# Where the softmax denominators of batches 4 to 7 are summed, in a fused attention and SwiGLU kernel on one Trainium2 core

## The chip, the cores and the metric

The kernel runs on one core of a Trainium2 chip. The core has a matrix engine (PE, with the loading of its stationary operand shown as PEld), a vector engine (DVE), a scalar engine (ACT), a general engine (POOL, also called GpSimd) and a queue engine (SP) that here only issues transfers. Each engine works through its own list of instructions in order, and the lists meet through semaphores. Matrix products go to PSUM, which has eight banks per partition. One bank holds 512 float32 values in each of 128 partitions.

The metric is the device time in microseconds (us) of one execution. The profile is of one other execution of the same program, with a span that is a little shorter than its own device time.

## The reference

Two blocks follow each other. The first is an attention with 32 memory slots per head, for 8 batches, 8 heads, 576 positions and a head size of 64:

```python
a = np.exp(phi - np.max(phi, axis=2, keepdims=True))
a = a / (np.sum(a, axis=2, keepdims=True) + 1e-09)      # over the 576 positions
k_m = np.einsum('bhsm,bhsd->bhmd', a, k)
v_m = np.einsum('bhsm,bhsd->bhmd', a, v)
scores = scale * np.matmul(q, k_m.transpose(0, 1, 3, 2))
attn = softmax(scores)                                   # over the 32 slots
out = np.matmul(attn, v_m)
```

The second is a SwiGLU layer over all 4608 tokens: `silu(x @ w_gate) * (x @ w_val) @ w_out`, with 512 model columns and 1536 inner ones. Inputs and output are float32.

What matters here is the division in the second line. For each head and slot one sum over 576 positions, the denominator, scales a row of `k_m` and of `v_m`.

## The kernel before

The kernel works on one batch after the other, in matrix products of bfloat16. For a batch it forms, in this order: the sums over positions ("key sums", though they hold keys and values: `kv_sum`, line 248, into two PSUM banks named `p_kv0` and `p_kv1`); their denominators (`kv_denominators`, line 293); the reciprocals of those (`kv_reciprocal`, line 301, on DVE, into `t_rS`); the scaled sums (`kv_norm`, lines 305 and 317, on DVE, into `t_bkv`); their transpose (`kv_T`, for batches 4 to 7 a transfer that SP issues, line 326). Then come the products of the value part with the two weight matrices (`p_u`, line 525), the scores (line 445), their softmax (multiplication at line 506, into `t_A`), and 24 slots per batch of a gate product and a value product (`p_g` and `p_v`, line 586), with the sigmoid unit on ACT (line 603) and a multiplication on DVE (line 609, into `t_h`). The output products (line 808) use sums of blocks that POOL and DVE prepare (lines 631 and 674).

The order on each engine is written out by hand. Batch b runs its 24 slots, and among these stand the next batch's key sums: `kv_items(b + 1, ...)` is put at slot 6 to 8, and its scaled sums are needed only by the products of `u_three` at slot 19 and by the next batch's scores. With the key sums, PE runs the last of batch b's own `p_u` products, in small tiles of the array (64 rows by 32 columns) that run beside each other. ACT and DVE copy these products out ("copies": at lines 552 and 556); `units` are four output products from a list that is left over.

A denominator is a product with two columns of ones. From batch 3 on POOL adds up the nine parts of exp(phi) first (`phi_sum`, lines 229 to 236: six operations), and leaves the sum as two bfloat16 parts in `t_ehl`, so that PE needs two matrix products for it (line 293), and not nine. Before that POOL waits, by a copy of one element (`wait_for`, line 716), until the softmax multiplication of head group 1 of batch `before` is done. `before` is the batch whose slots are running, so 2 for batch 3, 3 for batches 4 and 5, 5 for batch 6 and 6 for batch 7.

Where the denominators stand depends on the batch. For batches 3, 4, 6 and 7 (`behind`) they come after the key sums and the units, in two free columns (128 and 129) of `p_kv0`, and the reciprocal follows on DVE behind a copy of `p_u`. For batch 5 (`own`) they come ahead of the key sums, in a bank of their own, `p_S`, which is given back at once.

PSUM banks are handed out from a list of eight, first in, first out (`bank` and `done`). The order of the list is fixed when the program is built; a matrix product into a bank waits for the last reader of the bank's former contents.

Of the kernel before, what the change touches and what calls it, by code (L numbers as in the profile page):

```python
# [9 lines left out]
FP32 = mybir.dt.float32  # L10
# [4 lines left out]
def kernel(  # L15
# [28 lines left out]
    NG = 2  # L44
# [30 lines left out]
    def bank(shape, dtype, name):  # L75
        tag = free.pop(0)
        t = ps.tile(shape, dtype, tag=tag, name=name)
        held[id(t)] = tag, t
        return t

    def done(*tiles):

        for t in tiles:
            free.append(held.pop(id(t))[0])
# [27 lines left out]
    counted = (2,)  # L112
# [72 lines left out]
    ephis, rSs, bkvs, kTs, es, atts = {}, {}, {}, {}, {}, {}  # L185
# [34 lines left out]
    esums = {}  # L220

    def phi_sum(b, before):

        e = ephis[b].rearrange("p j i m -> p j (i m)")
        wait_for(atts[before, 1][0:1, 0, 0:1])
        t = att.tile([128, 4, 128], FP32, tag="es", bufs=1, name="t_es")
        add = lambda o, x, y: nc.gpsimd.tensor_tensor(out=o, in0=x, in1=y, op=ALU.add)
        add(t, e[:, 0:4], e[:, 4:8])  # L230
        add(t[:, 0:2], t[:, 0:2], t[:, 2:4])
        add(t[:, 0], t[:, 0], t[:, 1])
        add(t[:, 0], t[:, 0], e[:, 8])
        hl = att.tile([128, 2, 128], BF16, tag="ehl", name="t_ehl")
        nc.gpsimd.tensor_copy(out=hl[:, 0], in_=t[:, 0])
        nc.gpsimd.tensor_tensor(out=hl[:, 1], in0=t[:, 0], in1=hl[:, 0], op=ALU.subtract)
        esums[b] = hl
# [3 lines left out]
    def kv_sum(b, p, parts, among={}):  # L241


        w0, w1 = parts[0], parts[-1] + 1
        n = (w1 - w0 + (b in counted)) * D

        def one(i, g, j):
            nc.tensor.matmul(  # L248
                p[g][32 * i:32 * i + 32, 0:n],
                lhsT=phi_of(b, g, j, i),  # L250
                rhs=kv_of(b, slice(64 * g, 64 * g + 64), w0, w1, i, j),
                start=(j == 0),
                stop=(j == JK - 1),
                tile_position=(64 * g, 32 * i),
            )

        jobs = []
        for x, (i, g) in enumerate(TILES):
            at = 4 * x
            for j in range(JK + 1):  # L260
                for n_u, job in enumerate(among.get((i, g), ())):
                    if j == AHEAD[b][g][n_u][i]:
                        jobs.append((at, x, job))
                        at += 224
                if j < JK:
                    jobs.append((at, x, lambda i=i, g=g, j=j: one(i, g, j)))
                    at += 60
        run(x for _, _, x in sorted(jobs, key=lambda t: t[:2]))
# [5 lines left out]
    def kv_denominators(b, p):  # L274

        if b in masked:
            for g in range(NG):
                for j in range(JK):
                    nc.tensor.matmul(
                        p[:, g:g + 1],  # L280
                        lhsT=masked[b][:, j, g].rearrange("p i m -> p (i m)"),
                        rhs=ones1,
                        start=(j == 0),
                        stop=(j == JK - 1),
                    )
            return
        if b in esums:
            hl = esums.pop(b)
            terms = [hl[:, t] for t in range(2)]
        else:  # L290
            terms = [ephis[b][:, j].rearrange("p i m -> p (i m)") for j in range(JK)]
        for n, x in enumerate(terms):
            nc.tensor.matmul(p, lhsT=x, rhs=ones2, start=(n == 0), stop=(n == len(terms) - 1))

    def kv_reciprocal(b, p):
        r = att.tile([128, NG], FP32, tag="rS", name="t_rS")
        if b in counted:
            for g in range(NG):
                nc.vector.reciprocal(out=r[:, g:g + 1], in_=p[g][:, D:D + 1])
        else:  # L300
            nc.vector.reciprocal(out=r, in_=p)
        rSs[b] = r
# [4 lines left out]
    def kv_norm(b, p):  # L307

        t = att.tile([128, 3, 128], BF16, tag="bkv", name="t_bkv")
        flat = t.rearrange("p n x -> p (n x)")  # L310
        o = 2 * D if b in counted else D
        for g in range(NG):
            out = flat[:, 2 * D * g:].rearrange("p (a x) -> p a x", a=2)[:, :, D:2 * D]
            x = p[g][:, 0:2 * o].rearrange("p (a x) -> p a x", a=2)[:, :, 0:D]
            scaled_copy(out, x, rSs[b][:, g:g + 1])
            done(p[g])
        nc.vector.tensor_copy(out=t[:, 0:NG, 0:D], in_=t[:, 0:NG, D:2 * D])
        bkvs[b] = t

    def kv_T(b):  # L320


        kTs[b] = att.tile([128, 3, 128], BF16, tag="kT", name="t_kT")
        t = bkvs.pop(b)
        if b > 3:
            nc.sync.dma_start_transpose(out=kTs[b], in_=t.rearrange("p n x -> p (n x)"))
            return
        p = bank([128, 3, 128], BF16, "p_T")
        for n in (2, 0, 1):
            nc.tensor.transpose(p[:, n], t[:, n], ident)  # L330
        nc.vector.tensor_copy(out=kTs[b], in_=p)
        done(p)

    def kv_items(b, beside=None):


        def run_sums():
            o = 2 * D
            behind = b in esums and b != 5
            own = beside and not behind  # L340
            if own:
                d = bank([128, NG], FP32, "p_S")
                kv_denominators(b, d)
                kv_reciprocal(b, d)
                done(d)
            p = [bank([128, CH], FP32, f"p_kv{g}") for g in range(NG)]
            if beside:
                u, units = beside
                copies = u(lambda x: kv_sum(b, p, (0, 1), x))
                run(copies[:3])  # L350
            else:
                kv_sum(b, p, (0, 1))
            if behind:
                run(copies[3:5])
                units()
                kv_denominators(b, p[0][:, o:o + NG])
            if not own:
                kv_reciprocal(b, p if b in counted else p[0][:, o:o + NG])
            kv_norm(b, p)
            if behind:  # L360
                run(copies[5:])
            if own:
                run(copies[3:])
                units()

        return [run_sums, lambda: kv_T(b)]

    def direct(b, which):
# [344 lines left out]
    def wait_for(x):  # L713

        t = att.tile([1, 1], BF16, tag="mark", bufs=1, name="t_mark")
        nc.gpsimd.tensor_copy(out=t, in_=x)
# [236 lines left out]
    def run(items):  # L953
        for x in items:
            x()
# [155 lines left out]
    for b in range(2, B):  # L1111
        last = b + 1 == B
        exp_tables()
        if b == 2:
# [5 lines left out]
            sums = {n: f for n, f in zip(((1, 1), (0, 2), (1, 2)), late)}  # L1120
# [67 lines left out]
        beside = 0 if last else 2 if quad else min(4, len(backlog))  # L1188
# [5 lines left out]
        if not last:  # L1194
            if b > 2:
                load_qT(b + 1)
            for n in {3: (4, 5), 4: ()}.get(b, (b + 1,)):
                phi_sum(n, b)
            kvs_next = kv_items(b + 1, (u_beside(b), lambda: run(take(2))))
            streams += [  # L1200
                (kvs_next[:1], KV, KV + 2),
                (kvs_next[1:], KV + 2 + 2 * (b == 2), KV + 4 + 2 * (b == 2)),
                ([lambda: (u_three(b + 1), run(take(2)))], 19, 20),
            ]
        spread(*streams)
        flush_mul()
        units, ops = products(b, ("p1", "c11"))
# [35 lines left out]
```

## Time and profile before

| | |
|---|---|
| median of 3 runs | 231.25 us (231.09 to 231.45) |
| the profiled execution, its own device time | 231.05 us |
| span of the profile | 229.3 us, at full granted clock |
| busy share of PE, DVE, ACT, POOL | 96%, 81%, 75%, 66% |
| chain of work that ended last | 87% PE, 9% DMA |
| key sums of batch 4, 5, 6, 7 start at | 101.71, 127.68, 153.79, 177.54 us of the span |
| denominator products of batch 4, 5, 6, 7 start at | 103.26, 127.56, 155.34, 179.09 us |
| POOL done with the sum for batch 4, 5, 6, 7 | 102.32, 106.26, 154.49, 177.98 us |

The profile has a page with the busy time of each engine, the chain of work that ended last (followed back from the last instruction) and the costliest groups of instructions. From the same trace one can ask who waited for whom, and for a list of the instructions in order of time. A row of that list gives the start, the length of the row (of a run of equal instructions: from the first one's start to the last one's end), the engine, the line, the operation, what it writes and reads, and the count. A matrix product's end is modelled, so two rows of PE can overlap; the distance from start to start is what PE took.

### The profile page before, as it was taken

How to read it: one execution, taken by the hardware profiler on the slowest of the kernel's cores; microseconds unless marked ns; L12 is line 12 of the kernel's file. 1: busy time of each engine (PE TensorE's matmuls, PEld its weight loads, DVE VectorE, ACT ScalarE, POOL GpSimd, SP SyncE). 2: the span in 40 equal slices, each digit the busy share in tenths (PEclk: the TensorE clock that was granted, in tenths of full speed). 3: DMA queues.
4: the chain of work that ended last, by engine and by line, in shares of the span. 5: the costliest groups of instructions: out<-in, count | busy, mean ns of one | idle time of the engine just before them, and what ended most of it. 6: DMA issues, size and time to landing. Idle time of an engine off the chain costs nothing.

```text
span 229.3 us, 7221 instructions
## 1 busy us (share of the span) xinstructions
PE 220.2 (96%) x2826; PEld 170.5 (74%) x2826; DVE 186.7 (81%) x423; ACT 171.4 (75%) x365; POOL 151.8 (66%) x207
## 2 busy tenths in 40 slices
PE   6987899999999999999999999999999999999993
PEld 2544476778887876888788887888788878878893
DVE  4246699999977999999997768998999899977832
ACT  2868988988537898988875758978898889677311
POOL 8422737998099759979987788464845494039291
PEclk9999999999999999999999999999999999999999
DMA  6999999999994997999199955995114902202024
GB/s 212 209 210 206 198 207 207 208 258 266 207 195 118 248 279 154 230 204 195 72 219 197 177 175 124 256 226 94 38 56 115 105 0 96 91 0 94 23 92 164
DMA packets 36546, 36.84 MB, mean 161 GB/s; under 512 B 14496, under 2 KB 30880, under 8 KB 36512
## 3 DMA queue, kind: packets, MB, share of 16 engines
q0 software_dynamic: 16272, 22.42, 53.0%
q1 hardware_dynamic: 19568, 13.24, 22.7%
q10 hardware_dynamic: 672, 0.72, 0.9%
q8 instruction: 22, 0.36, 0.6%
q14 instruction: 12, 0.10, 0.1%
HBM read 42.47 MB, written 9.44 MB: 226 GB/s over the span
## 4 chain that ended last, share of the span: by engine, by line
PE 87%; DMA 9%; POOL 2%; issue 0%; ACT 0%; POOLq 0%; ACTq 0%
PE p_g L586 21%; PE p_v L586 21%; PE p_os L808 20%; PE p_oc L808 10%; DMA W<-in_moe_w_val_dram 9%; PE p_oa L808 5%; PE p_u L525 5%; PE p_kv L248 2%; PE p_os L796 1%; PE p_g L445 1%; POOL t_kv L101 1%; POOL t_kv L110 1%; POOL t_q L125 0%; PE p_q L432 0%; POOL W L155 0%
## 5 line engine op out<-in xcount | busy, mean ns | idle before, releaser
L609 DVE TENSOR_TENSOR t_h<-t_sg,p_v 128x288 bf16<-128x288 bf16 x192 | 82.1, 452 | 12.0 <-PE p_v L586 6.8
L586 PEld LDWEIGHTS <-t_U 128*128 128x128 bf16 x768 | 73.8, 98 | 19.9 <-issue 2.8
L603 ACT ACTIVATE t_sg<-p_g 128x288 bf16<-128x288 f32 x192 | 74.3, 420 | 18.4 <-PE p_g L586 12.0
L586 PE MATMUL p_g<-t_A,t_U 128*128 128x288 bf16 x384 | 77.0, 286 | 0.0
L586 PE MATMUL p_v<-t_A,t_U 128*128 128x288 bf16 x384 | 77.0, 286 | 0.0
L808 PEld LDWEIGHTS <-t_S 128*128 128x128 bf16 x384 | 37.3, 98 | 4.6 <-issue 0.2
L674 POOL TENSOR_TENSOR t_S<-t_h 128x512 bf16<-128x512 bf16 x17 | 19.7, 1157 | 23.3 <-DVE t_h L609 22.1
L808 PEld LDWEIGHTS <-t_h 128*128 128x128 bf16 x288 | 27.0, 98 | 7.3 <-issue 3.5
L552 ACT CAST t_U<-p_u 128x512 bf16<-128x512 f32 x50 | 26.4, 606 | 4.1 <-PE p_u L525 4.1
L808 PE MATMUL p_os<-t_T,t_S 128*128 128x256 bf16 x192 | 23.7, 273 | 0.0
L631 POOL TENSOR_TENSOR t_S<-t_S,t_h 128x512 bf16<-128x512 bf16 x17 | 19.6, 1155 | 1.3
L631 POOL TENSOR_TENSOR t_S<-t_h,t_S 128x512 bf16<-128x512 bf16 x16 | 18.4, 1154 | 0.0
L631 POOL TENSOR_TENSOR t_S<-t_h 128x512 bf16<-128x512 bf16 x16 | 18.4, 1152 | 0.0
L525 PE MATMUL p_u<-W,t_kT 64*32 64x512 bf16 (+1 forms) x416 | 16.5, 363 | 1.1 <-DVE t_kT L388 0.6
L556 DVE CAST t_U<-p_u 128x512 bf16<-128x512 f32 x22 | 14.3, 685 | 1.1 <-PE p_u L525 1.1
L808 PE MATMUL p_os<-t_T,t_h 128*128 128x256 bf16 x96 | 14.8, 274 | 0.0
L980 PE MATMUL p_warm<-bones 128*128 128x512 bf16 x44 | 12.6, 424 | 1.7 <-DVE bones L1002 1.7
L386 ACT COPY t_q<-p_os 128x512 f32<-128x512 f32 (+2 forms) x12 | 5.5, 470 | 9.2 <-PE p_os L796 5.1
L808 PE MATMUL p_oc<-t_T,t_S 128*128 128x256 bf16 x96 | 12.1, 273 | 0.0
L808 PE MATMUL p_oa<-WO,t_h 128*128 128x256 bf16 x96 | 11.8, 273 | 0.0
L808 PE MATMUL p_oc<-WO,t_S 128*128 128x256 bf16 x96 | 11.8, 273 | 0.0
L808 PE MATMUL p_os<-WO,t_h 128*128 128x256 bf16 x96 | 11.8, 273 | 0.0
(115 smaller groups left out, 329.4 us busy)
## 6 DMA issues: line engine op xcount, KB each, us to landing
out_dram<-t_o SPq DMA_DIRECT2D x11, 512.0 KB, 3.5
t_kv<-in_k_dram POOLq DMA_DIRECT2D x8, 576.0 KB, 10.7
t_q<-in_q_dram POOLq DMA_DIRECT2D x8, 576.0 KB, 8.2
t_kv<-in_v_dram POOLq DMA_DIRECT2D x8, 576.0 KB, 15.8
t_phi<-in_phi_dram POOLq DMA_DIRECT2D x6, 576.0 KB, 8.4
out_dram<-t_o SPq DMA_DIRECT2D x10, 256.0 KB, 7.4
WO<-in_moe_w_out_dram POOLq DMA_DIRECT2D x3, 512.0 KB, 19.2
W<-in_moe_w_gate_dram POOLq DMA_DIRECT2D x2, 512.0 KB, 16.2
```

The lines of the kernel that those rows point to most:

```text
L248: nc.tensor.matmul(p[g][32 * i:32 * i + 32, 0:n], lhsT=phi_of(b, g, j, i), rhs=kv_of(b, slice(64 * g, 64 * g + 64), w0, w1, i, j), start=( ...
L386: nc.scalar.copy(out=out, in_=in_)
L525: nc.tensor.matmul(p[g][32 * i:32 * i + 32, o:o + n], lhsT=kTs[b][64 * g:64 * g + 64, 2, 32 * i:32 * i + 32], rhs=w_part(w, c, i, g, halve ...
L552: nc.scalar.copy(out=t, in_=p)
L556: nc.vector.tensor_copy(out=t, in_=p)
L586: nc.tensor.matmul(p[:, 0:HALF], lhsT=Us[b, c, g][:, o // 2, which, 128 * (o % 2):128 * (o % 2 + 1)], rhs=atts[b, g][:, r], start=(g == 0) ...
L603: nc.scalar.activation(out=sg, in_=gate[:, 0:HALF], func=AF.Silu)
L609: nc.vector.tensor_tensor(out=dst, in0=sg, in1=val[:, 0:HALF], op=ALU.mult)
L631: eng.tensor_tensor(out=out, in0=x, in1=y, op=ALU.subtract)
L674: eng.tensor_tensor(out=t[:, 0], in0=A21, in1=A22, op=ALU.add)
L808: nc.tensor.matmul(mine[home][:, u], lhsT=lhs(c, m, u), rhs=rhs(c, m), start=fresh and u == 0, stop=(k == 5), skip_group_check=u == 1 or n ...
L980: nc.tensor.matmul(p[:, 0:128 * a], lhsT=bones, rhs=x.to_broadcast([128, a, 128]) if a > 1 else bones, start=True, stop=True,)
```

## The change

The diff is whole:

```diff
@@ phi_sum(b, before)
-        wait_for(atts[before, 1][0:1, 0, 0:1])
+        wait_for(atts[before, b < 4][0:1, 0, 0:1])
@@ kv_items(b, beside), run_sums
             o = 2 * D
-            behind = b in esums and b != 5
-            own = beside and not behind
-            if own:
-                d = bank([128, NG], FP32, "p_S")
-                kv_denominators(b, d)
-                kv_reciprocal(b, d)
-                done(d)
             p = [bank([128, CH], FP32, f"p_kv{g}") for g in range(NG)]
+            sums = p[0][:, o:o + NG]
+            if b > 3:
+                kv_denominators(b, sums)
+                kv_reciprocal(b, sums)
             if beside:
                 u, units = beside
                 copies = u(lambda x: kv_sum(b, p, (0, 1), x))
-                run(copies[:3])
+                n = {3: 5, 5: 3}.get(b, 4)
+                run(copies[:n])
+                if b != 5:
+                    units()
             else:
                 kv_sum(b, p, (0, 1))
-            if behind:
-                run(copies[3:5])
-                units()
-                kv_denominators(b, p[0][:, o:o + NG])
-            if not own:
-                kv_reciprocal(b, p if b in counted else p[0][:, o:o + NG])
+            if b == 3:
+                kv_denominators(b, sums)
+            if b <= 3:
+                kv_reciprocal(b, p if b in counted else sums)
             kv_norm(b, p)
-            if behind:
-                run(copies[5:])
-            if own:
-                run(copies[3:])
+            if beside:
+                run(copies[n:])
+            if b == 5:
                 units()
```

For batches 4, 6 and 7 the two denominator products and the reciprocal move from behind the key sums to ahead of them, into the same two columns of `p_kv0` as before. For batch 5 they stay ahead of the key sums, and move from a bank of their own into those columns. For batches 4 to 7 POOL's sums wait for the softmax multiplication of head group 0, and no longer for that of group 1. The orders of copies and units, and all of batches 2 and 3, are what they were. No instruction is added or removed.

## The prediction

> **What bounds the kernel now.** I read the page first, then the list of waits, then the list of instructions in order of time around each of the four key sums.
>
> ```profile
> span 229.3 us, 7221 instructions
> ...
> PE 220.2 (96%) x2826; PEld 170.5 (74%) x2826; DVE 186.7 (81%) x423; ACT 171.4 (75%) x365; POOL 151.8 (66%) x207
> ...
> PE 87%; DMA 9%; POOL 2%; issue 0%; ACT 0%; POOLq 0%; ACTq 0%
> ```
>
> PE bounds it: the chain is PE from 26.6 us on, when the weights have landed. In the waits PE itself appears with what happens before that, like the first line here; later it waits some hundredths at most:
>
> ```profile
> PE p_warm L980 <- DVE bones L1002: 1.7, 1, 1.7
> ...
> DVE t_rS L301 <- PE p_kv L293: 0.7, 3, 0.2
> ```
>
> The last line (total, times, longest in us) is the only wait that the old place of the denominators makes: DVE idles 0.7 us in three batches. It is DVE's idle time, and PE does not wait for what follows. So a microsecond saved on DVE here is worth nothing, and one that PE loses is lost in full, unless PE loses less later; from 82 us to 223 us I find no wait of PE above 0.03 us that could shrink.
>
> Batch 6 stands for 4 and 7 as well:
>
> ```profile
> 151.52 2.90 DVE L609 TENSOR_TENSOR t_h<-t_sg,p_v 128x288 bf16<-128x288 bf16 x6
> ...
> 153.45 0.41 PE L586 MATMUL p_v<-t_A,t_U 128*128 128x288 bf16 x2
> ...
> 153.79 0.30 PE L248 MATMUL p_kv<-t_kv,t_ephi 64*32 64x128 bf16 x16
> ...
> 154.89 0.61 PE L808 MATMUL p_os<-t_T,t_h 128*128 128x256 bf16 x4
> ...
> 155.34 0.19 PE L293 MATMUL p_kv<-ones,t_ehl 128*128 128x2 bf16 x2
> ...
> 155.39 0.41 PE L586 MATMUL p_g<-t_A,t_U 128*128 128x288 bf16 x2
> 155.57 0.17 DVE L301 RECIPROCAL t_rS<-p_kv 128x2 f32<-128x2 f32 x1 [0.24 <-PE p_kv L293]
> ```
>
> What to see: when PE starts the key sums at 153.79, DVE is not done with the six multiplications. The sixth reads the value product that PE issued last, at 153.45, and ends at 151.52 + 2.90 = 154.42, 0.63 us into the key sums. DVE trails PE by that much, by nature of the pair.
>
> Batch 5 already has its denominators ahead, in a bank of their own:
>
> ```profile
> 127.56 0.19 PE L293 MATMUL p_S<-ones,t_ehl 128*128 128x2 bf16 x2
> 127.61 0.45 DVE L609 TENSOR_TENSOR t_h<-t_sg,p_v 128x288 bf16<-128x288 bf16 x1 [0.26 <-PE p_v L586]
> ...
> 127.68 0.36 PE L248 MATMUL p_kv<-t_kv,t_ephi 64*32 64x128 bf16 x24
> ...
> 127.98 0.16 DVE L301 RECIPROCAL t_rS<-p_S 128x2 f32<-128x2 f32 x1
> ...
> 128.13 0.40 PE L525 MATMUL p_u<-W,t_kT 64*32 64x512 bf16 x4
> ...
> 128.79 0.61 PE L808 MATMUL p_os<-t_T,t_h 128*128 128x256 bf16 x4
> ...
> 129.23 0.41 PE L586 MATMUL p_g<-t_A,t_U 128*128 128x288 bf16 x2
> ```
>
> Here the reciprocal comes 0.30 us after the key sums have begun, and nobody minds: another bank.
>
> **The change, part by part.**
>
> The new wait. The changed program, as built, gives each semaphore wait. In batches 4, 5, 6 and 7 the first key-sum product into `p_kv0`, right behind the two denominator products, waits for a DVE count, and the count is the one that this batch's reciprocal brings when it is done. In the program before, the same product waits for an older multiplication, long finished. So although the columns are free, the bank's next writer is held until its reader is done. PE takes its products in order; everything behind, the other key sums, the `p_u` products, the units and the next slots, is held too. And DVE works in order: the reciprocal stands behind the sixth multiplication.
>
> The reciprocal's time. In batch 5 it starts at 127.98, which is 0.08 before the end of the multiplication ahead of it (127.61 + 0.45 = 128.06), and takes 0.16 (0.17 in the other batches). A finished DVE instruction is seen by PE about 0.06 later: the multiplication that ends at 128.06 is followed at 128.13 by a `p_u` product that waits for it, 0.07; single rows in batch 3 show 0.05. So the key sums can start at the last multiplication's end - 0.08 + 0.17 + 0.06, that is 0.15 after it:
> - batch 6: 154.42 + 0.15 = 154.57, was 153.79: 0.78 later;
> - batch 4: six multiplications from 99.44, 2.90 long, end at 102.34, so 102.49, was 101.71: 0.78;
> - batch 7: from 175.27, end 178.17, so 178.32, was 177.54: 0.78;
> - batch 5: 127.98 + 0.16 + 0.06 = 128.20, was 127.68: 0.52.
>
> Together 2.86 us of PE. Bounds: below, the wait costs nothing (the reciprocal is always done in time: excluded if the order on DVE holds, and kept as a rival); above, 1.0 for each of the three if the start after a wait pays once more for the change of array tiles, seen as 0.34 from 153.45 over two products of 0.12 to 153.79, that is 0.10 extra, and the reciprocal waits another 0.1 for PE. I take the middle, as it is made of rows for the same instructions.
>
> The old place. From 154.89 PE takes 0.50 for four output products and the denominators; in batch 5 the same four without denominators take 129.23 - 128.79 = 0.44. So 0.06 goes, in three batches: -0.18. At the new place the pair costs nothing more, as it lies inside the wait (batch 5: key sums start 0.12 after the pair; the bare change of tiles takes 0.10).
>
> POOL's sums. In batch 6 POOL's copy starts at 150.49, 0.12 after the two multiplications at line 506 (one row, 148.98 + 1.39 = 150.37), and the six sums end at 154.49. Half of 1.39 sooner gives 153.79. Then the second product's weights (0.10), the product (0.17) and two hand-overs of 0.06 to 0.1: DVE could start the reciprocal at about 154.2, and it is busy until 154.34. So POOL is covered, by 0.1 us. In batch 7 the sums end at 177.98 - 0.70 = 177.28, ahead of the key sums; in batch 4 the waited-for multiplication is POOL's own, POOL would go on at 97.20 and not at 98.31, and end at 101.21, also ahead. If POOL were not sooner, see below. The sums now run beside DVE's second multiplication; at 96.62 DVE's transpose (0.77) ran beside POOL's own multiplication no slower than the one at 148.28 (0.78) without it, so I take 0; at worst 0.4 us for each of batches 6 and 7, since the slots' first product needs it 0.14 to 0.4 later.
>
> Batch 5's bank. One bank less is taken, and all later products use other banks in turn. The list still hands out the one freed longest ago; no PE wait for a bank above 0.03 us shows after 82 us. Price 0, bounds -0.1 and +0.1.
>
> DVE loses the idle 0.24 before the reciprocal, and the scaled sums follow the copy directly. They feed SP's transpose at 156.91, landing in about 3 us, needed at 162.36: 2 us in hand, worth 0.
>
> Sum: 2.86 - 0.18 = 2.68 us. On the profiled execution's 231.05 (span 229.3 and 1.75 around it) this makes 233.73; that execution lies 0.20 below the median of 231.25, which would give 233.93. I say 233.8.
>
> **What the skill says.** The Trainium skill, PSUM — Partial Sum Buffer, section "PSUM bank collisions raise a hardware error", wants PSUM guarded by bank and quadrant and not by address: different columns of one bank still collide. By that rule the new wait is no accident of the build, and free columns are no free place; a reading by address would leave the sum at -0.18. No trace here can show a collision. The Trainium skill, TensorE: Matmul & The Clock Gate, Part 1, has PE's clock halved after an idle window of about 3.4 us; such a drop, from the rows, is the last rival below.
>
> **The rivals.**
> 1. No wait in effect (the other side: not slower). It decides if the reciprocal is done by the time that the key sums could start, so if DVE were within 0.1 us of PE there. For it: PE's program apart from this wait is lighter by 0.18, less 0.02 at each new place. Against: the rows show DVE 0.63 behind in all three batches. It gives 231.05 - 0.12 = 230.9, no change that can be told. Chance 0.06.
> 2. POOL becomes the late one: its sums do not come sooner (slowed by DVE, or the copy is held by something else). Then the low part comes at 154.49 in batch 6, the reciprocal starts at 154.49 + 0.06 + 0.10 + 0.17 + 0.10 = 154.92 and not at 154.34: 0.58 more. Batch 7: 178.41 for 178.09, 0.32; batch 4: 102.75 for 102.26, 0.49. It gives 233.73 + 1.4 = 235.1. Against: POOL waited 2.72 and 2.74 us idle for that multiplication in batches 6 and 7. Chance 0.08.
> 3. PE's clock drops after the gaps. The granted clock is 9 tenths or more in every slice, and in the tuned part PE never pauses as long as 0.3 us, so no row shows what a pause of 0.8 does. One slice of the page (229.3 / 40 = 5.7 us) at half clock, after one gap, would cost 2.9 us and give 236.6. Chance 0.03. By the figure of the Trainium skill, TensorE: Matmul & The Clock Gate, Part 1, a pause of 0.8 us is far short of an idle window, and the price is nothing.
>
> **The numbers.** My forecast has 0.83: 233.8, by its own bounds 233.2 to 234.6. To leave no more than 2 in 10 out, the range takes in rival 2 and a stall a third smaller: 232.9 to 235.1. A measurement of this kernel tells about 0.2%, 0.46 us, from no change. Slower takes the forecast and rivals 2 and 3, 0.94 together. Rival 1 is split into 0.05 for the same and 0.01 for faster, as no part of the sum reaches 0.46 us below zero.
>
> **What would show it.** In the changed kernel's waits there is a new line: PE's key-sum product waiting for the reciprocal, four times, some 2.3 us in total (the gap less the pair itself). From the last value product to the first key sum it should be 1.12 and not 0.34 in batches 4, 6 and 7. The reciprocal directly follows the sixth multiplication. Four output products and the next gate take 0.44. POOL's copy for batch 6 comes 0.7 sooner against the slots. I am wrong if the key sums start on time, if PE makes up the gap before the next batch, or if a gap of more than 1 us points to POOL.

## The result, and the profile after

The changed kernel takes 234.40 us (median of 4 runs, 234.36 to 234.46) against 231.28 us before (231.09 to 231.45). The ratio is 1.0135, with a 95% interval of 1.0118 to 1.0153: 3.1 us slower. The profiled execution of the changed kernel took 234.46 us, that of the kernel before 231.05, so the two traces lie 3.4 us apart, 0.3 more than the medians.

The page of the changed kernel, its first lines and its chain:

```profile
span 232.6 us, 7221 instructions
...
PE 221.0 (95%) x2826; PEld 171.3 (74%) x2826; DVE 187.5 (81%) x423; ACT 171.2 (74%) x365; POOL 152.9 (66%) x207
...
PE 76%; DMA 9%; DVE 5%; POOL 4%; ACT 3%; issue 2%; DVEq 0%; POOLq 0%; ACTq 0%
```

PE does the same 2826 products, but the chain that ended last has gone from 87% PE to 76%: it now passes through DVE, POOL and ACT. The list of waits (total, times, longest, in us) says where PE is held:

```profile
PE p_kv L248 <- DVE t_rS L301: 1.8, 4, 0.7
...
PEld L293 <- POOL t_ehl L236: 0.7, 2, 0.4
...
PE p_g L583 <- DVE t_A L503: 0.4, 1, 0.4
PE p_kv L293 <- POOL t_ehl L236: 0.3, 1, 0.3
```

None of these lines was there before. The first is the forecast wait. The second and last are POOL's low part in batches 6 and 7. The third is a gate product that waits for a softmax multiplication, and was not forecast.

Batch 4, in order of time, changed kernel:

```profile
101.49 1.44 DVE L606 TENSOR_TENSOR t_h<-t_sg,p_v 128x288 bf16<-128x288 bf16 x3
...
101.95 0.41 PE L583 MATMUL p_v<-t_A,t_U 128*128 128x288 bf16 x2
...
102.20 0.19 PE L293 MATMUL p_kv<-ones,t_ehl 128*128 128x2 bf16 x2
102.84 0.16 DVE L301 RECIPROCAL t_rS<-p_kv 128x2 f32<-128x2 f32 x1
...
103.06 0.30 PE L248 MATMUL p_kv<-t_kv,t_ephi 64*32 64x128 bf16 x16 [0.67 <-DVE t_rS L301]
...
104.16 0.61 PE L805 MATMUL p_os<-t_T,t_h 128*128 128x256 bf16 x4
...
104.61 0.41 PE L583 MATMUL p_g<-t_A,t_U 128*128 128x288 bf16 x2
```

The last multiplication ends at 101.49 + 1.44 = 102.93, the reciprocal begins 0.09 before that, ends at 103.00, and the key sums start at 103.06. From the last value product to the first key sum it is 1.11 us; before it was 0.34. Four output products and the next gate take 0.45, not 0.50.

To see what each place costs I took the same PE product in both traces and followed how much later it starts. The lateness is constant to 0.01 us between the places below and jumps at them:

| place | forecast, us | in the trace, us |
|---|---|---|
| start of the tuned part (weights landing) | - | +0.06 |
| first gate of the slots in which batch 4's key sums stand | 0 | +0.52 |
| key sums of batch 4 | +0.78 | +0.77 |
| key sums of batch 5 | +0.52 | +0.52 |
| key sums of batch 6 | +0.78 | +0.91 |
| key sums of batch 7 | +0.78 | +0.76 |
| old place of the denominators, three batches | -0.18 | -0.16 |
| sum | +2.68 | +3.38 |

Nothing is given back later.

### The profile page after: what moved, and what is told of

The parts are those of the page before. It is cut to its first block, busy times and chain, and to the rows that moved or that the text cites. A ratio compares the mean times of both kernels' runs of the same rounds, so it can differ in the third digit from the quotient of the medians.

```text
span 232.6 us, 7221 instructions
## 1 busy us (share of the span) xinstructions
PE 221.0 (95%) x2826; PEld 171.3 (74%) x2826; DVE 187.5 (81%) x423; ACT 171.2 (74%) x365; POOL 152.9 (66%) x207
## 4 chain that ended last, share of the span: by engine, by line
PE 76%; DMA 9%; DVE 5%; POOL 4%; ACT 3%; issue 2%; DVEq 0%; POOLq 0%; ACTq 0%
PE p_g L583 19%; PE p_v L583 18%; PE p_os L805 17%; DMA W<-in_moe_w_val_dram 9%; PE p_oc L805 8%; PE p_u L522 5%; PE p_oa L805 4%; DVE t_h L606 2%; PE p_kv L248 2%; POOL t_es L229 1%; PE p_os L793 1%; ACT t_E L453 1%; DVE t_o L843 1%; ACT t_U L549 1%; PE p_g L442 1%
```

## The experiments

The theory after this reading has three parts. First, the denominators stand in the bank that the key sums go to, so the key sums wait for the reciprocal, and through it for whatever DVE or POOL finishes last. Second, POOL's earlier start helps less than it should in batch 6. Third, the same earlier start puts POOL's first addition beside a DVE multiplication in batch 4, and one holds the other. The rivals are that the place ahead of the key sums costs by itself, that the bank list does, or that the early sums are a pure loss. The table gathers the lateness at each place, in us, from the traces as above (without the start of the tuned part), and the medians less that of the kernel before on the same chip (231.28 for the changed kernel, 231.31 for e1 to e4, 231.08 for e5 and e6, 231.15 for e7 and e8, 231.18 for e9).

| kernel | first gate | batch 4 | batch 5 | batch 6 | batch 7 | old place | sum | medians |
|---|---|---|---|---|---|---|---|---|
| changed | 0.52 | 0.77 | 0.52 | 0.91 | 0.76 | -0.16 | 3.32 | +3.12 |
| e1, late POOL | 0 | 1.09 | 0.52 | 1.19 | 0.91 | -0.16 | 3.55 | +3.61 |
| e2, early POOL alone | 0.50 | 0 | 0 | 0 | 0 | 0 | 0.50 | +0.44 |
| e3, own bank | 0.51 | 0.03 | 0 | 0.57 | 0.32 | -0.16 | 1.27 | +1.20 |
| e4, batch 5 alone | 0 | 0 | 0.52 | 0 | 0 | 0 | 0.52 | +0.37 |
| e5, reciprocal first | 0.50 | 0.36 | 0.33 | 0.91 | 0.66 | -0.16 | 2.60 | +2.70 |
| e6, early for 6 and 7 | 0 | 1.08 | 0.52 | 0.91 | 0.77 | -0.16 | 3.12 | +3.30 |
| e7, e2 with half additions | 0.63 | 0 | 0 | 0 | 0 | 0 | 0.63 | +0.62 |
| e8, e2 again | 0.50 | 0 | 0 | 0 | 0 | 0 | 0.50 | +0.44 |
| e9, e2 with chained additions | 0 | 0 | 0 | 0 | 0 | 0 | 0 | -0.06 |

### e3: a bank of its own

```diff
+            if b > 3:
+                d = bank([128, NG], FP32, "p_S")
+                kv_denominators(b, d)
+                kv_reciprocal(b, d)
+                done(d)
             p = [bank([128, CH], FP32, f"p_kv{g}") for g in range(NG)]
             sums = p[0][:, o:o + NG]
-            if b > 3:
-                kv_denominators(b, sums)
-                kv_reciprocal(b, sums)
```

> The changed kernel, with the denominators of batches 4 to 7 in a bank of their own, given back before the key sums take theirs. Theory (the bank is what holds the key sums): no key-sum product waits for the reciprocal. What is left is 0.52 at batch 4's gate, and POOL's low part: 0.56 in batch 6 and 0.30 in batch 7 directly on PE; less 0.03 to 0.05 per batch at the old place: 1.25 over the kernel before, 232.5 us. Rival (the place ahead of the key sums is what costs, whatever the bank): 234.4 us.

Measured: 232.51 us, ratio 1.0053 (1.0041 to 1.0065). Batch 4 in this kernel's list in order of time:

```profile
101.92 1.44 DVE L608 TENSOR_TENSOR t_h<-t_sg,p_v 128x288 bf16<-128x288 bf16 x3
...
102.63 0.19 PE L293 MATMUL p_S<-ones,t_ehl 128*128 128x2 bf16 x2
102.75 0.30 PE L248 MATMUL p_kv<-t_kv,t_ephi 64*32 64x128 bf16 x16
...
103.27 0.16 DVE L301 RECIPROCAL t_rS<-p_S 128x2 f32<-128x2 f32 x1
```

The reciprocal stands behind DVE's multiplications as in the changed kernel, and the key sums run 0.52 ahead of it. The order on PE and DVE is that of the changed kernel; only the bank differs. So the shared bank, with the wait that the program as built puts on it, is the cause, and the place is nearly free: 0.03 us in batch 4. No run here keeps the shared bank and leaves the wait out, so whether the columns could be shared without it is not shown. What is left in batches 6 and 7 is PE waiting for POOL's low part, without DVE in between:

```profile
154.77 0.43 POOL L236 TENSOR_TENSOR t_ehl<-t_es,t_ehl 128x128 bf16<-128x128 f32 x1
155.25 0.10 PEld L293 LDWEIGHTS <-t_ehl 128*128 128x128 bf16 x1 [0.41 <-POOL t_ehl L236]
155.25 0.18 PE L293 MATMUL p_S<-ones,t_ehl 128*128 128x2 bf16 x1 [0.33 <-POOL t_ehl L236]
155.36 0.30 PE L248 MATMUL p_kv<-t_kv,t_ephi 64*32 64x128 bf16 x16
```

### e4: batch 5 alone

In the kernel before, batch 5's denominators lose their own bank.

```diff
-            if own:
-                d = bank([128, NG], FP32, "p_S")
-                kv_denominators(b, d)
-                kv_reciprocal(b, d)
-                done(d)
             p = [bank([128, CH], FP32, f"p_kv{g}") for g in range(NG)]
+            if own:
+                kv_denominators(b, p[0][:, o:o + NG])
+                kv_reciprocal(b, p[0][:, o:o + NG])
```

> The kernel before, with one thing changed: batch 5's denominators, which already stand ahead of its key sums, go into columns 128 and 129 of the first key-sum bank. Theory: its key sums start 0.52 us later, nothing else, 231.8 us. Rival (only the moved ones cost, or one bank less in the list gives it back): 231.3 us.

Measured: 231.68 us, ratio 1.0018 (1.0009 to 1.0026). It is the same cost the other way round: one bank less, 0.52 us at one place of the trace, and nothing at any other. The medians differ by 0.37, a little less than the trace; the bank list gives nothing that a trace shows.

### e5: the reciprocal ahead of the last multiplication

The changed kernel, with the DVE half of one value product put off.

```diff
-            nc.vector.tensor_tensor(out=dst, in0=sg, in1=val[:, 0:HALF], op=ALU.mult)
-            done(val)
...
+            def finish():
+                nc.vector.tensor_tensor(out=dst, in0=sg, in1=val[:, 0:HALF], op=ALU.mult)
+                done(val)
...
+            if b in (3, 4, 5, 6) and s == KV - 1:
+                put_off.append(finish)
+            else:
+                finish()
...
                 kv_reciprocal(b, sums)
+                put_off.pop()()
```

> The changed kernel, with one DVE instruction moved: in batches 4 to 7 the multiplication of the last value product ahead of the key sums stands behind the reciprocal and no longer ahead of it. Theory (PE waits for the reciprocal, and that waits for this multiplication where POOL is in time): the key sums of batch 4 start 0.37 late and not 0.76, those of batch 5 0.34 and not 0.52, batch 7 gains about 0.1, until POOL's low part is the limit, batch 6 nothing, as POOL is the limit there: 0.7 less than the changed kernel, 233.7 us. Rival (the wait has a fixed price wherever the reciprocal stands on DVE): 234.4 us.

Measured: 233.78 us, ratio 1.0114 (1.0097 to 1.0131). By place it is as the theory has it: 0.36 in batch 4 (0.37 expected), 0.33 in batch 5 (0.34), 0.66 in batch 7, batch 6 unmoved because POOL is the limit there. Together 0.7 us less than the changed kernel. The medians, taken against the kernel before on each chip, give 0.4 less. Batch 4 here:

```profile
102.26 0.19 PE L293 MATMUL p_kv<-ones,t_ehl 128*128 128x2 bf16 x2
102.49 0.17 DVE L301 RECIPROCAL t_rS<-p_kv 128x2 f32<-128x2 f32 x1
102.58 0.43 DVE L609 TENSOR_TENSOR t_h<-t_sg,p_v 128x288 bf16<-128x288 bf16 x1
102.71 0.31 PE L248 MATMUL p_kv<-t_kv,t_ephi 64*32 64x128 bf16 x16 [0.26 <-DVE t_rS L301]
```

This is the wait with nothing ahead of the reciprocal but the denominators: from them to the key sums 0.45 us, in place of 0.12 in e3. So a reader in the bank has a floor of about 0.33 us here, and what DVE has queued ahead of it, or POOL's late low part, made the rest.

### e1: POOL's sums as late as before

```diff
-        wait_for(atts[before, b < 4][0:1, 0, 0:1])
+        wait_for(atts[before, 1][0:1, 0, 0:1])
```

> The changed kernel, but POOL's sums wait for the softmax multiplication of head group 1 again. Theory (the key sums wait for the reciprocal, and the reciprocal for POOL's low part where that is late): the gate of batch 4's slots is on time again (-0.52), but POOL's sums end at the old places, and the key sums start 0.50 us after them: 1.10 late in batch 4, 1.19 in batch 6, 0.93 in batch 7, and 0.52 in batch 5 as now; less 0.16 at the old place, 3.6 us over the kernel before, so 234.9 us. Rival (beginning POOL's sums sooner is only a loss, and the key sums wait for DVE alone): 0.52 less than the changed kernel, 233.9 us.

Measured: 234.92 us, ratio 1.0153 (1.0139 to 1.0167). The gate is on time, and the key sums wait for POOL: 1.09, 1.19 and 0.91 us late (1.10, 1.19 and 0.93 expected). The rival's 233.9 is out. The wait's price is set by whichever of DVE and POOL is done last.

### e6: early sums for batches 6 and 7 only

```diff
-        wait_for(atts[before, b < 4][0:1, 0, 0:1])
+        wait_for(atts[before, b < 6][0:1, 0, 0:1])
```

> The changed kernel, with POOL's sums for batches 4 and 5 waiting for head group 1 again, those for 6 and 7 as changed. Theory: batch 4's gate is on time (-0.52), but its sum ends 0.6 us later and the key sums start 1.10 late and not 0.76 (+0.34): 0.18 less than the changed kernel, 234.2 us. Rival (the early start in batch 4 pays for its collision in full): 234.4 us or more.

Measured: 234.38 us, ratio 1.0141 (1.0126 to 1.0156), whose interval overlaps that of the changed kernel. The medians don't tell the two apart, and the time is the rival's 234.4, not the 234.2 expected. The trace has the gate on time (-0.52) and batch 4's key sums 1.08 late and not 0.77 (+0.31), as expected; the 0.2 us that this leaves between the traces does not show in the medians.

### e2 and e8: the early sums alone

The kernel before, with the changed line of `phi_sum` and nothing else.

```diff
-        wait_for(atts[before, 1][0:1, 0, 0:1])
+        wait_for(atts[before, b < 4][0:1, 0, 0:1])
```

> The kernel before, with the earlier start of POOL's sums alone. Theory (in batch 4 POOL's first addition and DVE's multiplication of head group 1 read at the same time and the later one is held): that multiplication takes 1.60 us and not 0.76, the first gate of the slots is 0.52 us late, nothing else changes: 231.8 us. In batches 6 and 7 POOL's one-element copy is held instead (0.58 and not 0.18), which costs nothing here. Rival (the held multiplication has to do with the moved denominators): 231.3 us, multiplication 0.76.

> The same kernel as in the second run, beside the split one on the same chip: both theories expect its first gate of batch 4 0.50 us late and 231.75 us.

Measured: 231.75 us, ratio 1.0016 (1.0007 to 1.0024), and again 231.59 us, ratio 1.0018 (1.0008 to 1.0027). From e2's list:

```profile
96.81 0.77 DVE L496 STREAM_TRANSPOSE t_lz<-t_z 128x576 f32<-128x576 f32 x1
...
97.42 1.15 POOL L229 TENSOR_TENSOR t_es<-t_ephi 128x512 f32<-128x512 bf16 x1
...
97.61 1.58 DVE L506 TENSOR_TENSOR t_A<-t_E,t_lz 128x576 bf16<-128x576 bf16 x1
98.62 0.29 PE L586 MATMUL p_g<-t_A,t_U 128*128 128x288 bf16 x1
98.64 1.66 POOL L229 TENSOR_TENSOR t_es<-t_es 128x256 f32<-128x256 f32 x2
...
99.24 0.53 PE L586 MATMUL p_g<-t_A,t_U 128*128 128x288 bf16 x3 [0.34 <-DVE t_A L506]
```

The multiplication takes 1.58 us; without POOL beside it, it took 0.76. It starts 0.19 after POOL's addition, POOL is done at 98.57, and the multiplication ends at 99.19, 0.62 later. It is held for about as long as POOL's addition runs, and then needs 0.62 of its 0.76. Its row shows no idle time: it is just long. POOL's next two additions take 1.66 in place of 1.26: it is held in turn. And PE's first gate waits for the result.

### e7: POOL's first addition in two halves

The kernel of e2, and this besides:

```diff
-        add(t, e[:, 0:4], e[:, 4:8])
+        for n in ((0, 2), (2, 4)) if b == 4 else ((0, 4),):
+            add(t[:, n[0]:n[1]], e[:, n[0]:n[1]], e[:, 4 + n[0]:4 + n[1]])
```

> The kernel before with the earlier sums alone, as in the second run, and with the first addition of batch 4's sum split into two of half its size. Theory (the engine that comes second is held until the other's instruction ends, and then runs at its own speed): the softmax multiplication on DVE is held only by the first half, so it ends about 0.6 us after that half and takes about 1.1 us and not 1.6; the first gate is late by less than 0.1 us, and POOL's second half is held in its turn: 231.3 us. Rival (both engines share a path and slow each other in proportion, for as long as they overlap): the multiplication still takes about 1.6 us and the gate is 0.5 us late, 231.75 us.

Measured: 231.77 us, ratio 1.0025 (1.0015 to 1.0036).

```profile
97.49 1.28 POOL L229 TENSOR_TENSOR t_es<-t_ephi 128x256 f32<-128x256 bf16 x2
...
97.68 1.71 DVE L507 TENSOR_TENSOR t_A<-t_E,t_lz 128x576 bf16<-128x576 bf16 x1
```

My theory failed here: the multiplication was not let in between the halves, and took 1.71. It ends 0.62 after the second half (97.49 + 1.28 = 98.77, and 99.39). The rival's number is near, but sharing in proportion does not explain why the end is 0.62 after POOL's end in both kernels. The halves don't depend on each other, and POOL runs them without a pause. In e2 DVE got in where POOL's second addition needs the first, after a pause of 0.08 us. That gave the next run.

### e9: additions that depend on each other

The kernel of e2, and this besides:

```diff
+        if b == 4:
+            add(t[:, 0:2], e[:, 0:2], e[:, 4:6])
+            add(t[:, 0:2], t[:, 0:2], e[:, 2:4])
+            add(t[:, 0:2], t[:, 0:2], e[:, 6:8])
+        else:
             add(t, e[:, 0:4], e[:, 4:8])
             add(t[:, 0:2], t[:, 0:2], t[:, 2:4])
```

> The kernel before with the earlier sums alone, and batch 4's sum begun as three additions of 256 columns, each on the result of the one before, in place of one of 512 and one of 256. Theory, mended after the split run (DVE is let in only where POOL pauses, which it does between additions that depend on each other, by about 0.08 us, and not between independent ones): the softmax multiplication ends about 0.62 us after the first addition, so it takes about 1.1 us and not 1.57 or 1.71, the first gate is late by less than 0.1 us, and POOL's second addition is held in turn: 231.2 us. Rival (DVE is held for as long as POOL has additions of this kind waiting): 1.7 us or more, the gate 0.5 us late or more, 231.6 us.

Measured: 231.12 us, ratio 0.9999 (0.9990 to 1.0008): the loss is gone.

```profile
97.32 0.66 POOL L229 TENSOR_TENSOR t_es<-t_ephi 128x256 f32<-128x256 bf16 x1
...
97.50 1.10 DVE L511 TENSOR_TENSOR t_A<-t_E,t_lz 128x576 bf16<-128x576 bf16 x1
98.06 1.83 POOL L229 TENSOR_TENSOR t_es<-t_es,t_ephi 128x256 f32<-128x256 f32 x2
98.51 0.67 PE L591 MATMUL p_g<-t_A,t_U 128*128 128x288 bf16 x4
```

The first addition is as short as e7's halves, 0.66, but now the next one has to wait for it. The multiplication ends at 98.60, 0.62 after the first addition's end, and the gate runs without a break.

No kernel here beats the kernel before. What could be won at the old place is 0.05 us a batch, less than a measurement tells.

## Why the prediction was right, and what it mis-sized

The direction, the place and the main mechanism were right, and the time fell in the range. I said 233.8 us; it was 234.4. That this still lies within my own bounds, 233.2 to 234.6, is in part luck: the room above was meant for a dearer wait and for DVE held in batches 6 and 7, and what used it up was DVE held in batch 4. How the upper bound was made is not worked out either: the terms' own upper bounds add up to 235.3 (233.73 + 3 x 0.22 + 2 x 0.4 + 0.1).

- The new wait. It stands in the waits four times, 1.8 us in total and not 2.3, since in batches 6 and 7 PE waits a part of the time for POOL's low part. From the last value product to the first key sum it is 1.11, 1.25 and 1.10 us in batches 4, 6 and 7 (1.12 forecast). The four terms, 0.78, 0.52, 0.78 and 0.78, came out as 0.77, 0.52, 0.91 and 0.76. e3 shows that the bank makes it, e5 that it moves with the reciprocal's place on DVE, e4 that it costs batch 5 the same without any other part of the change.
- The old place: -0.18, measured -0.16.
- "So POOL is covered, by 0.1 us" failed in batch 6. POOL was expected 0.70 us sooner, and was 0.27 sooner: its first addition starts at 152.17, 0.15 ahead of the first gate product at 152.32, where before it started at 150.63, 0.12 behind that product at 150.51. The one-element copy ahead of it ran beside DVE's second softmax multiplication and took longer:

```profile
150.78 1.38 DVE L503 TENSOR_TENSOR t_A<-t_E,t_lz 128x576 bf16<-128x576 bf16 x2
...
151.63 0.58 POOL L713 COPY t_mark<-t_A 1x1 bf16<-1x1 bf16 x1 [2.05 <-DVE t_A L503]
...
152.17 1.15 POOL L229 TENSOR_TENSOR t_es<-t_ephi 128x512 f32<-128x512 bf16 x1
```

  The copy took 0.58 us and not 0.18, and the addition came right after DVE was done at 152.16. Thus the low part was the last to come, the reciprocal waited for it and not for DVE, and batch 6 lost 0.13 more:

```profile
156.07 0.18 PE L293 MATMUL p_kv<-ones,t_ehl 128*128 128x2 bf16 x1 [0.33 <-POOL t_ehl L236]
156.29 0.17 DVE L301 RECIPROCAL t_rS<-p_kv 128x2 f32<-128x2 f32 x1
156.51 0.30 PE L248 MATMUL p_kv<-t_kv,t_ephi 64*32 64x128 bf16 x16 [0.26 <-DVE t_rS L301]
```

- "The sums now run beside DVE's second multiplication ... so I take 0" is the term that was most mis-sized: 0.52 us, in batch 4. The row I priced it by was DVE's transpose beside POOL's multiplication, 0.77 with and 0.78 without. It was the wrong row: the two overlap by 0.16 us only (POOL's ends at 95.50 + 1.28 = 96.78), and the transpose reads one operand from SBUF (the on-chip memory of every tile here whose name does not begin with `p_`). The multiplication at line 506 reads two. No row of the kernel before has this multiplication beside POOL's additions, which is what the old wait had kept apart. But its trace has other DVE rows with two operands in SBUF beside POOL rows, and they are longer than their like:

```profile
54.95 1.62 POOL L663 COPY t_x<-t_h 128x256 bf16<-128x256 bf16 x3
55.00 0.69 DVE L631 TENSOR_TENSOR t_S<-t_S,t_h 128x512 bf16<-128x512 bf16 x1
55.61 0.64 DVE L631 TENSOR_TENSOR t_S<-t_h 128x512 bf16<-128x512 bf16 x1
...
143.78 0.42 DVE L631 TENSOR_TENSOR t_S<-t_S,t_h 128x512 bf16<-128x512 bf16 x1
144.13 0.42 DVE L631 TENSOR_TENSOR t_S<-t_h 128x512 bf16<-128x512 bf16 x1
```

  The same two subtractions take 0.69 and 0.64 us beside POOL's copies, and 0.42 without. These rows could have told before any run that the term need not be 0. I had given the bound, 0.4 us, to batches 6 and 7, and none to batch 4, where POOL starts first. The Trainium skill, SBUF — State Buffer, section "SBUF: two separate sides", states the case: a DVE instruction with two SBUF inputs and a GpSimd one that reads SBUF use one port pair, and the one that starts first keeps it. By that rule, as an estimate from rows of the kernel before: POOL's addition of 1.15 us, begun at about 97.3, holds DVE until about 98.45; its 0.76 and a hand-over of 0.05 then put at 99.26 the gate product that stood at 98.56, 0.7 us late. Measured were 0.52, as DVE needs only 0.62 after POOL's end. The runs agree with the rule but for one point, below.
- Rival 1, no wait in effect, is out by the waits. Rival 2, POOL late, came true in small, 0.13 us in batch 6; e1 shows it in full. Rival 3, a lower clock, did not come: the granted clock is 1.0 over the span.

Of the 0.70 us by which the trace's sum exceeds the forecast's, the collision (0.52) and batch 6 (0.13) are nearly all.

## What to carry to other kernels

Free columns are not a free place if another engine has to read them before the bank's next writer may go on: what the writer then waits for is the reader's whole queue, and it is worth listing what stands ahead of the reader on its engine. A wait that keeps two engines apart may be there for the sake of a shared path and not for the data, so before it is loosened the two instructions that it lets meet have to be named and their operands compared with the row that prices them. And a row that is longer than its like with no idle time before it is a wait all the same.

## What was not expected of the hardware

A DVE multiplication with both inputs in SBUF was held while POOL's additions ran, in one case past the end of the first of them: 1.71 us with two independent additions of 0.66 back to back (e7), 1.10 with one of 0.66 and a dependent one 0.08 behind it (e9), 1.58 with one of 1.15 (e2), 0.76 with none. In each it ended 0.62 us after POOL's pause began. The Trainium skill's section named above speaks of the instruction that started first; in e7 the hold lasted through two.

That DVE is let in only where POOL pauses, as e9's expectation has it, is not so everywhere. In the kernel before, three copies on POOL, each of another block of `t_h`, ran beside three subtractions on DVE with both inputs in SBUF (the first two are shown above):

```profile
54.95 0.50 POOL L663 COPY t_x<-t_h 128x256 bf16<-128x256 bf16 x1
...
55.34 0.68 POOL L663 COPY t_x<-t_h 128x256 bf16<-128x256 bf16 x1
...
55.94 0.64 POOL L663 COPY t_x<-t_h 128x256 bf16<-128x256 bf16 x1
...
56.17 0.64 DVE L631 TENSOR_TENSOR t_S<-t_h,t_S 128x512 bf16<-128x512 bf16 x1
```

The copies end at 55.45, 56.02 and 56.58, and the subtractions at 55.69, 56.25 and 56.81: the engines took turns, though each of POOL's rows begins before the one ahead of it ends. What decides between the two cases is open. A copy reads one operand and an addition two, and the additions of e9 differ from those of e7 also in what they read (its second one reads float32 sums), so e9 does not separate the pause, the dependency and the kind of operand.

A DVE row with one operand in PSUM was not held: the one at line 846 that writes `t_o` from `p_os` and `t_p` took 0.68 us at 98.70 in the kernel before, beside POOL's addition of 1.15 begun at 98.46, and 0.69 at 198.22 with nothing on POOL. That the shared port pair is the cause was not measured by itself; the runs show who held whom, and for how long.
